# Beacon keys transposed in fp32, batch 0's first keys and queries handled apart, its last pair loaded ahead of v

## The chip, the cores and the metric

The kernel runs on one core of a Trainium2 chip. The metric is the device time of one execution in microseconds. The kernel before takes 338.09 us (median of four runs, 337.98 to 339.79). The profile shows one execution on the chip; its times are counted from the start of the execution's span.

## The reference

Causal attention with 16 extra "beacon" keys and values per head, then an MLP with a squared ReLU:

```
B, H, S, Nb, D = 8, 8, 576, 16, 64
k_all = concat([beacon_k, k], axis=2); v_all = concat([beacon_v, v], axis=2)
scores = q @ k_all.T / sqrt(D)          # beacons are seen by all, k is causal
a = softmax(scores)
attn = a @ v_all                        # (B, H, S, D)
x = attn as (B*S, H*D) = (4608, 512)
out = square(relu(x @ w_in)) @ w_out    # w_in 512 x 2048, w_out 2048 x 512
```

All inputs and the output are fp32. The kernel computes in bf16 and accumulates in fp32.

## The kernel before

The work is a pipeline of eight batches. Two heads make a pair (four pairs a batch), and their 2 x 64 columns fill TensorE's 128 rows. For a pair, q and k are brought into transposed form (`qT`, `kT`, with the 16 beacon keys first), TensorE writes scores into PSUM (line 620), ScalarE takes the exponential into `pt` (lines 629 and 671), VectorE masks the diagonal blocks by a minimum with `tri` (lines 712 and 716), TensorE multiplies with v, which has a column of ones that gives the softmax sum (line 738), and VectorE divides by that sum (lines 755 and 757). The result is transposed to `xT`: for batches 0 to 2 on TensorE (line 805) with an evacuation by ScalarE or VectorE, later by DMA (line 788). The MLP runs over nine chunks of 512 tokens: `x @ w_in` (line 901), ReLU by ScalarE or VectorE (lines 917 and 919), a square by VectorE (line 926), and `@ w_out` (line 939, the last rows line 851).

How data come in differs by batch:

- Batch 0, pair 0: two parts (240 and 336 tokens), loaded in fp32 by SP (k) and ACT (q) into `osb` (line 522), cast to bf16 by VectorE (k) and ScalarE (q), transposed on TensorE (line 481), and evacuated from PSUM by VectorE (line 327). For the first part k and q share one PSUM bank and one planned operation.
- Batch 0, pairs 1 to 3, and batch 1: loads on POOL's queue that also cast (line 449), transposed on TensorE (line 484).
- From batch 2 on: loads into staging buffers `stg` on SP's queue (lines 370 and 371), casts on POOL (line 327), and two transposing DMAs per batch (line 404).
- Beacon keys of batches 0 and 1: a load on SP (line 416), a cast to bf16 on VectorE (line 419), four small transposes on TensorE (line 429), and an evacuation into `kT` by VectorE.
- v: loads to `stg` on POOL's queue for batches 0 and 1, on SP's later, then casts into `vb` (line 327).
- Weights: DMAs with a cast on POOL's queue (lines 830 and 838), four pieces each.

The order of instructions on every engine is written at build time by a list scheduler (class `Order`). Each operation has a planned duration, a priority, dependencies, and pools that it takes from: two double PSUM strips for scores (`strip`), four PSUM banks (`ps`) for everything else, and eight staging buffers. `late` is an allowance that is added to the planned time at which TensorE may count on an operation. `behind` fixes the order of two operations. The plan only sets the order: on the chip each engine takes its instructions in that order and waits for semaphores. Until the planned 22 us, TensorE is given matmuls on zeros ("fillers", line 295) where the plan has nothing for it.

Names that the change touches: `SOFT` is the order of POOL's first loads (`p3k` is pair 3's k, `v0` a v tile, `w0` a piece of w_in, `t0` and `t1` halves of the mask). `RANK` is the order in which batch 0's eight phases (pair, part) are scored. `PLAN` says, for batches 1 to 7, how many 512-column pieces of scores are issued together: a 2 uses the two strips, a 3 two PSUM banks besides. `add_beacon` has the beacon path, `add_strided` the transposes, `add_first_loads` pair 0's loads and casts.

Of the kernel before, what the change touches and what calls it, by code (L numbers as in the profile page):

```python
# [9 lines left out]
FP32 = mybir.dt.float32  # L10
# [36 lines left out]
class Order:  # L47
# [22 lines left out]
    def run(self):  # L70
# [16 lines left out]
        free = {e: 2.3 if e == "DVE" else 0.0 for e in engines}  # L87
        dma_free = 0.0
        lanes = {"SP": [], "POOL": [], "ACT": []}
        events = [(0.0, 0, None, None)]  # L90
# [4 lines left out]
        while events:  # L95
# [19 lines left out]
            while again:  # L115
                again = False
                for e in engines:
# [26 lines left out]
                    if best is None:  # L144
                        if e == "PE" and 0.3 < now < self.FILL_UNTIL and self.pools["ps"]:
                            cols = 128 if now < 7.0 else 256
                            free[e] = now + 0.107
                            issued.append((Op("fill", "PE", 0.107, lambda e, cols=cols, bank=self.pools["ps"][0]: self.fill(bank, cols)), e, now))
                            seq += 1
                            heapq.heappush(events, (free[e], seq, "free", None))  # L150
                        continue
# [51 lines left out]
def kernel(  # L203
# [29 lines left out]
    def sb(name, shape, dt):  # L233
        return pool.tile(shape, dt, name=name)
# [32 lines left out]
    bkf = [sb("bkf", [Nb, H, D], FP32)] * 2  # L267
    bks = [sb(f"bks{i}", [Nb, H, D], BF16) for i in range(2)]
# [45 lines left out]
    ident_op = add("ident", "POOL", 1.3, lambda e: make_identity(nc, ident), prio=-300.0)  # L314
    tri_ops = [add(f"tri{i}", "POOL", (0.95, 0.55)[i], lambda e, i=i: emit_tri(e, i), prio=-250.0) for i in range(2)]
# [39 lines left out]
    def add_load(b, x, c, prio, behind=[], sync=[]):  # L355
# [34 lines left out]
        if x != "v":  # L390
            if b < NPE + 2:
                deps += [zero_ops[b]]
            else:
# [4 lines left out]
                            late=(5.0 if b else 1) if x == "v" else 0.0)  # L398

    def add_trans(b, x, prio):  # L400
        srcb, dst = (qb, qT) if x == "q" else (kb, kT)

        def emit(e):
            nc.sync.dma_start(
                out=dst[b % 2].rearrange("p g (c t) -> p (g c) t", c=NT),
                in_=srcb[b % 2].rearrange("p g c d -> p (g c d)"),
                transpose=True,
            )

        deps = [cast[b, x, c] for c in range(NT)]  # L410
        deps += [o for p in range(HP * (b - 2), HP * (b - 1)) for o in qk_ops[p]]
        trans[b, x] = [add(f"tr{b}{x}", "SP", 4.1, emit, prio=prio, deps=deps, dma=3.7, late=3.0)]

    def add_beacon(b, prio):
        prio = prio if b else -299.5
        ld = add(f"bkl{b}", "SP", 0.45, lambda e: [nc.sync.dma_start(
            out=bkf[b % 2], in_=beacon_k[b].transpose([1, 0, 2]))], prio=prio, dma=0.1,
                 deps=[cast[b - 1, "bk"]] if b else [])
        bk = add(f"bkc{b}", "DVE", 0.4, lambda e: nc.vector.tensor_copy(bks[b % 2], bkf[b % 2]), prio=prio,
                 deps=[ld])  # L420
        cast[b, "bk"] = bk
        if b:
            bk.need.extend(norm_ops[HP - 1, 0])
        box = {}

        def emit_tp(e):
            pp = ps[box["t"].held[2]].bitcast(BF16)
            for pr in range(HP):
                nc.tensor.transpose(pp[:, pr * Nb:(pr + 1) * Nb], bks[b % 2][:, 2 * pr:2 * pr + 2, :], ident[0:Nb, 0:Nb])

        busy = [o for pr in range(HP) for o in qk_ops[HP * (b - 2) + pr]] if b >= 2 else []
        box["t"] = add(f"tpb{b}", "PE", 0.25, emit_tp, prio=prio - 100.0, deps=[bk, ident_op], take=("ps", "tp"))

        def emit_ev(e):
            pp = ps[box["t"].held[2]].bitcast(BF16)
            copy_on(e, kT[b % 2][:, :, 0:Nb], pp[:, 0:HP * Nb].rearrange("p (g n) -> p g n", g=HP))

        bk_ev[b] = add(f"ekb{b}", "DVE", 0.2, emit_ev, prio=-200.0, deps=[box["t"]] + busy, give=box["t"])

    bk_ev = {}  # L440

# [17 lines left out]
    def add_strided(b, prio):  # L459
# [7 lines left out]
        for part, (t0, np_, ns, prs) in enumerate(parts_of[b]):  # L467
            n_tok = np_ * ns
            own = b == 0 and part < 2
            for pr in prs:  # L470
                groups = ["kq"] if 2 * n_tok <= 1024 else ["k", "q"]
                for n, xs in enumerate(groups):
# [20 lines left out]
                    for i, x in enumerate(xs):  # L493
# [6 lines left out]
                        if b == 0:  # L500
                            engs = ("DVE",)
                        else:
                            engs = ("DVE",) if x == "k" else ("DVE", "ACT")
                        ev = add(f"e{x}{b}.{part}.{pr}", engs,
                                 {"DVE": 0.12 + n_tok / 960.0, "ACT": 0.2 + n_tok / 1200.0}, emit_ev,
                                 prio=(-200.0 if x == "k" else -199.0) + 0.01 * part, deps=[tp])
# [5 lines left out]
    def add_first_loads():  # L512
        first = []
        at = 0
        for part in range(2):
            t0, np_, ns, _ = parts_of[0][part]
            for n, (x, t) in enumerate((("k", k), ("q", q))):
# [3 lines left out]
                def emit(e, t=t, n=n, raw=raw, t0=t0, np_=np_, ns=ns):  # L521
# [3 lines left out]
                o = add(f"fld{x}{part}", ("SP", "ACT")[n], (0.45, 0.55)[n], emit, prio=-300.0 + part,  # L525
                        dma={"k": (0.3, 0.75), "q": (0.55, 0.65)}[x][part])
                first.append(o)

                def emit_cast(e, x=x, raw=raw, part=part):
                    copy_on(e, paired_buf(x, part).rearrange("p s (u d) -> p u s d", u=2), raw)  # L530

                strided[0, part, 0, x] = add(f"fc{x}{part}", ("DVE", "ACT")[n],
                                             ((0.33, 0.75)[part], (0.42, 0.52)[part])[n], emit_cast,
                                             prio=-210.0 + part, deps=[o], late=0.3)
# [63 lines left out]
    RANK = [(0, 0), (0, 1), (1, 0), (2, 0), (1, 1), (3, 0), (2, 1), (3, 1)]  # L598
# [37 lines left out]
    PLAN = ((2,2,3,3,3),(2,2,3,3,3),(2,3,3,3,2),(2,3,3,3,2),(2,3,3,3,2),(2,3,3,3,2),(2,3,3,3,2))  # L636
# [339 lines left out]
    SOFT = "t0 p1k p1q t1 p2k p2q v0 v1 p3k p3q v2 v3 v4 w0 w1 w2 w3".split()  # L976
# [94 lines left out]
```

The softmax here doesn't subtract the row's maximum and nothing guards it: scores larger than these inputs give would overflow.

## Time and profile before

| What | Value |
|---|---|
| Median of four runs | 338.09 us (337.98 to 339.79) |
| The profiled execution | 337.98 us, its span 336.3 us |
| TensorE (PE) busy | 331.3 us, 99% of the span |
| ScalarE (ACT) busy | 191.2 us, 57% |
| VectorE (DVE) busy | 170.2 us, 51% |
| GpSimd (POOL) busy | 93.1 us, 28% |
| First scores of batch 0 start | 6.82 us |
| Last exponential of batch 0 ends | 22.98 us |
| First matmul with w_in starts | 23.12 us |
| First matmul with w_out starts | 44.37 us |

How to read it: in the busy time an engine's row gives what it executed, and a matmul's duration includes its way through the array, so consecutive matmuls overlap and a busy TensorE may still be waiting for its next instruction. "[0.58 <-PE strip L620]" behind a row says how long the engine had stood idle and what released it. The chain of work follows the last instruction back to what released it, step by step. A row of the busy time by stretches has the length, then for PE, weight loads, DVE, ACT and POOL the busy time with the number of instructions in brackets, the granted clock, the mean share of the DMA engines that is busy, and GB/s. In a row of the groups of instructions the count stands behind an x, then busy time and mean ns of one.

### The profile page before, as it was taken

The page shows a single profiled execution, that of the slowest core. Times are in us where ns is not written, and L with a number is a line of the kernel's source. Part 1 is how long each engine was busy: PE and PEld are TensorE (multiplying, and loading weights), DVE is VectorE, ACT ScalarE, POOL GpSimd, SP SyncE. Part 2 cuts the span into 40 slices and gives each one's busy share as a digit, 9 for nine tenths or more (in the row PEclk, how much of TensorE's full clock was granted, in tenths as well). Part 3 has the DMA queues.
Part 4 walks back from the last instruction along what each step waited for, and adds up shares of the span by engine and source line. Part 5 has one row for each costly group of instructions (what it writes and reads, how often), then busy time and mean ns, then how long its engine had stood idle before and what let it go on. Part 6 is the DMA issues. An engine that isn't in the chain of part 4 may idle for free.

```text
span 336.3 us, 7856 instructions
## 1 busy us (share of the span) xinstructions
PE 331.3 (99%) x3197; PEld 188.5 (56%) x3197; DVE 170.2 (51%) x389; ACT 191.2 (57%) x291; POOL 93.1 (28%) x145
## 2 busy tenths in 40 slices
PE   8999999999999999999999999999999999999996
PEld 7577765544654555555458845554555544444444
DVE  4786885248545983477147823573457302301400
ACT  3886765377647836566467556676457216515621
POOL 9874712406504614041134231424000000000000
PEclk9999999999999999999999999999999999999999
DMA  8999998999999999799699997998210231011003
GB/s 148 186 204 217 207 161 189 241 232 211 205 209 244 188 176 187 178 240 168 143 227 235 180 187 171 254 193 167 90 62 2 46 90 62 0 62 65 1 0 126
DMA packets 143955, 51.74 MB, mean 154 GB/s; under 512 B 130702, under 2 KB 138798, under 8 KB 143918
## 3 DMA queue, kind: packets, MB, share of 16 engines
q1 hardware_dynamic: 135375, 42.19, 61.5%
q0 software_dynamic: 7904, 8.69, 15.0%
q8 instruction: 25, 0.41, 0.5%
q10 hardware_dynamic: 639, 0.36, 0.4%
q14 instruction: 12, 0.10, 0.1%
HBM read 37.22 MB, written 9.44 MB: 139 GB/s over the span
## 4 chain that ended last, share of the span: by engine, by line
PE 89%; DMA 6%; POOL 4%; issue 0%; ACT 0%; POOLq 0%
PE ps L939 36%; PE ps L901 36%; PE ps L738 8%; PE strip L620 5%; DMA qk_area<-in_q_dram 4%; PE ps L620 2%; DMA stg<-in_v_dram 2%; POOL qk_area L449 1%; PE ps L851 1%; POOL w_in L830 1%; POOL vb L327 1%; PE ps L805 1%; PE ps L484 0%; POOL tri L311 0%; POOL stg L371 0%; POOL stg L370 0%
## 5 line engine op out<-in xcount | busy, mean ns | idle before, releaser
L901 PE MATMUL ps<-xT,w_in 128*128 128x512 bf16 (+3 forms) x704 | 134.3, 340 | 0.0
L939 PE MATMUL ps<-w_out,g 128*128 128x512 bf16 x560 | 130.5, 379 | 0.0
L901 PEld LDWEIGHTS <-w_in 128*128 128x128 bf16 x704 | 65.3, 98 | 51.5 <-issue 0.7
L917 ACT ACTIVATE g<-ps 128x512 bf16<-128x512 f32 (+2 forms) x118 | 66.3, 562 | 42.4 <-PE ps L901 41.8
L629 ACT ACTIVATE pt<-strip 128x1024 bf16<-128x1024 f32 (+3 forms) x86 | 81.4, 1004 | 13.2 <-PE strip L620 13.0
L926 DVE TENSOR_TENSOR g<-g 128x1024 bf16<-128x1024 bf16 (+2 forms) x80 | 52.6, 666 | 63.4 <-ACT g L917 62.4
L939 PEld LDWEIGHTS <-g 128*128 128x128 bf16 x560 | 51.6, 98 | 56.8 <-issue 1.7
L327 POOL CAST qk_area<-stg 128x512 bf16<-128x512 f32 (+2 forms) x60 | 41.4, 697 | 59.3 <-DMA stg<-in_k_dram 32.1
L325 ACT COPY osb<-ps 128x512 f32<-128x512 f32 (+2 forms) x29 | 16.4, 568 | 65.1 <-PE ps L939 60.5
L327 POOL CAST vb<-stg 128x512 bf16<-128x512 f32 (+1 forms) x40 | 26.0, 660 | 73.1 <-DMA stg<-in_v_dram 67.7
L738 PEld LDWEIGHTS <-pt 128*128 128x128 bf16 (+1 forms) x960 | 36.1, 98 | 10.2 <-DVE pt L712 0.4
L738 PE MATMUL ps<-vb,pt 128*128 128x65 bf16 (+1 forms) x960 | 39.0, 194 | 0.0
L712 DVE TENSOR_TENSOR pt<-pt,tri 128x512 bf16<-128x512 bf16 x64 | 28.4, 452 | 12.2 <-ACT pt L629 6.6
L757 DVE TENSOR_TENSOR xn<-ps,rcp 128x320 bf16<-128x320 f32 (+2 forms) x64 | 31.5, 492 | 2.3
L919 DVE TENSOR_SCALAR g<-ps 128x512 bf16<-128x512 f32 (+2 forms) x42 | 24.7, 605 | 13.1 <-PE ps L901 12.3
L671 ACT ACTIVATE pt<-ps 128x512 bf16<-128x512 f32 x42 | 22.8, 597 | 13.7 <-PE ps L620 11.1
L620 PEld LDWEIGHTS <-kT 64*128 64x128 bf16 x596 | 19.8, 94 | 16.0 <-issue 14.2
L755 DVE RECIPROCAL rcp<-ps 128x5 f32<-128x5 f32 (+2 forms) x64 | 12.2, 191 | 31.1 <-PE ps L738 30.2
L620 PE MATMUL strip<-qT,kT 64*128 64x208 bf16 (+13 forms) x474 | 27.0, 239 | 0.0
L327 DVE COPY osb<-ps 128x512 f32<-128x512 f32 (+1 forms) x9 | 5.8, 647 | 33.1 <-PE ps L939 21.3
L295 PE MATMUL ps<-g 128*128 128x128 bf16 (+1 forms) x83 | 10.6, 284 | 1.1 <-DVE warm L302 1.1
L716 DVE TENSOR_TENSOR pt<-pt,tri 80x160 bf16<-80x160 bf16 x32 | 10.8, 338 | 0.0
(42 smaller groups left out, 97.8 us busy)
## 6 DMA issues: line engine op xcount, KB each, us to landing
out_dram<-osb SPq DMA_DIRECT2D x17, 512.0 KB, 4.6
stg<-in_q_dram SPq DMA_DIRECT2D x24, 256.0 KB, 5.0
stg<-in_k_dram SPq DMA_DIRECT2D x18, 256.0 KB, 5.3
stg<-in_v_dram SPq DMA_DIRECT2D x18, 256.0 KB, 4.8
w_in<-in_moe_w_in_dram POOLq DMA_DIRECT2D x4, 512.0 KB, 7.9
w_out<-in_moe_w_out_dram POOLq DMA_DIRECT2D x4, 512.0 KB, 11.1
stg<-in_v_dram POOLq DMA_DIRECT2D x6, 256.0 KB, 7.9
stg<-in_k_dram SPq DMA_DIRECT2D x6, 224.0 KB, 4.3
```

What stands on the lines that cost most here:

```text
L327: eng[e].tensor_copy(dst, src)
L620: nc.tensor.matmul(st[hj][:, at:at + t1 - t0], kT[b % 2][hp, pr, 128 * c:128 * c + 128], qT[b % 2][hp, pr, t0:t1], start=True, stop=True,)
L629: nc.scalar.activation(pt[:, :, at:at + width], strips[qk.slots[s]][:, :, 0:width], AF.Exp, bias=0.0, scale=scale)
L671: nc.scalar.activation(pt[:, hj, at:at + 512], ps[qk.wide[hj]], AF.Exp, bias=0.0, scale=scale)
L712: nc.vector.tensor_tensor(out=d, in0=d, in1=tri[:, m0:m0 + m, :][:, None].to_broadcast([128, 2, m, 128]), op=ALU.min)
L738: nc.tensor.matmul(a[:, at + (t - tl[0]) * (D + 1):at + (t - tl[0] + 1) * (D + 1)], P[0:rr, hj, o:o + 128], vb[b % 2][0:rr, c, 2 * pr + hj ...
L757: nc.vector.tensor_tensor(out=xn[b % 2].rearrange("p t (h d) -> p h t d", d=D)[:, h0:h0 + nh, tl[0]:tl[0] + nt], in0=a[:, :, :, 0:D], in1= ...
L901: nc.tensor.matmul(h[:, lo - spans[0][0]:hi - spans[0][0]], w_in_sb[:, mc, ft * 128:(ft + 1) * 128], xT[:, mc, lo % RING:lo % RING + hi - lo],
L917: nc.scalar.activation(dst, h, AF.Relu, bias=0.0, scale=1.0)
L919: nc.vector.tensor_scalar(out=dst, in0=h, scalar1=0.0, scalar2=None, op0=ALU.max)
L926: nc.vector.tensor_tensor(out=d, in0=d, in1=d, op=ALU.mult)
L939: nc.tensor.matmul(o, G[:, fc, ts * 128:(ts + 1) * 128], w_out_sb[:, fc, :], start=(fc == 0), stop=(fc == NFT - 1))
```

## The change

- The beacon keys of batches 0 and 1 are no longer cast. TensorE transposes them in fp32 against a 16x16 fp32 identity, which VectorE makes once by a copy; the evacuation converts them to bf16. The next beacon load waits for the transposes instead of the cast, and batch 1's transposes wait for what its cast waited for. Batch 0's beacon load stands behind k's second part on SP instead of ahead of it.
- Pair 0's first part: k and q are transposed into two PSUM banks as operations of their own. The evacuation of q's second part may run on ScalarE. Some planned durations, allowances and priorities of these operations are new; pair 1 to 3's evacuations in batch 0 get a priority 500 higher, and k's second cast may run on either engine.
- Pair 3's k and q go ahead of all v tiles on POOL's queue.
- Pair 1's second phase is scored ahead of pair 2's first one.
- Batch 2's scores are issued in groups of 2 (and a last 1), without the groups of 3.
- Allowances: 3.0 instead of 5.0 for v casts of batches 1 and 2, 1.5 instead of 3.0 for batch 2's transposing DMAs.
- Fillers begin at a planned 0.9 us instead of 0.3; they widen from 128 to 256 columns at a planned 6.0 instead of 7.0. The plan for ACT starts at 0.05.

```diff
-        free = {e: 2.3 if e == "DVE" else 0.0 for e in engines}
+        free = {e: {"DVE": 2.3, "ACT": 0.05}.get(e, 0.0) for e in engines}
...
-                        if e == "PE" and 0.3 < now < self.FILL_UNTIL and self.pools["ps"]:
-                            cols = 128 if now < 7.0 else 256
+                        if e == "PE" and 0.9 < now < self.FILL_UNTIL and self.pools["ps"]:
+                            cols = 128 if now < 6.0 else 256
...
-    bkf = [sb("bkf", [Nb, H, D], FP32)] * 2
-    bks = [sb(f"bks{i}", [Nb, H, D], BF16) for i in range(2)]
+    bkf = sb("bkf", [Nb, H, D], FP32)
+    ident32 = sb("ident32", [Nb, Nb], FP32)
...
+    ident32_op = add("ident32", "DVE", 0.1, lambda e: nc.vector.tensor_copy(ident32, ident[0:Nb, 0:Nb]), prio=-300.0, deps=[ident_op])
...
-                            late=(5.0 if b else 1) if x == "v" else 0.0)
+                            late=(5.0 if b > 2 else 3.0 if b else 1) if x == "v" else 0.0)
...
-        trans[b, x] = [add(f"tr{b}{x}", "SP", 4.1, emit, prio=prio, deps=deps, dma=3.7, late=3.0)]
+        trans[b, x] = [add(f"tr{b}{x}", "SP", 4.1, emit, prio=prio, deps=deps, dma=3.7, late=3.0 if b > 2 else 1.5)]
...
-        prio = prio if b else -299.5
+        prio = prio if b else -298.5
...
-                 deps=[cast[b - 1, "bk"]] if b else [])
-        bk = add(f"bkc{b}", "DVE", 0.4, lambda e: nc.vector.tensor_copy(bks[b % 2], bkf[b % 2]), prio=prio,
-                 deps=[ld])
+                 deps=[bk_tp[b - 1]] if b else [])
...
-            pp = ps[box["t"].held[2]].bitcast(BF16)
             for pr in range(HP):
-                nc.tensor.transpose(pp[:, pr * Nb:(pr + 1) * Nb], bks[b % 2][:, 2 * pr:2 * pr + 2, :], ident[0:Nb, 0:Nb])
+                nc.tensor.transpose(ps[box["t"].held[2]][:, pr * Nb:(pr + 1) * Nb], bkf[:, 2 * pr:2 * pr + 2, :], ident32)
...
-        box["t"] = add(f"tpb{b}", "PE", 0.25, emit_tp, prio=prio - 100.0, deps=[bk, ident_op], take=("ps", "tp"))
+        box["t"] = bk_tp[b] = add(f"tpb{b}", "PE", 0.25, emit_tp, prio=prio - 100.0,
+                                  deps=[ld, ident32_op] + (norm_ops[HP - 1, 0] if b else []), take=("ps", "tp"))
...
-                groups = ["kq"] if 2 * n_tok <= 1024 else ["k", "q"]
+                groups = ["kq"] if 2 * n_tok <= 1024 and not own else ["k", "q"]
...
-                            engs = ("DVE",)
+                            engs = ("ACT", "DVE") if own and part == 1 and x == "q" else ("DVE",)
...
-                                 prio=(-200.0 if x == "k" else -199.0) + 0.01 * part, deps=[tp])
+                                 prio=(-200.0 if x == "k" else -199.0) + 0.01 * part - (500.0 if b == 0 and part == 2 else 0.0), deps=[tp])
...
-                strided[0, part, 0, x] = add(f"fc{x}{part}", ("DVE", "ACT")[n],
-                                             ((0.33, 0.75)[part], (0.42, 0.52)[part])[n], emit_cast,
-                                             prio=-210.0 + part, deps=[o], late=0.3)
+                strided[0, part, 0, x] = add(f"fc{x}{part}", (("DVE",), ("ACT",))[n] if part == 0 or x == "q" else ("ACT", "DVE"),
+                                             {"DVE": (0.46, 0.6)[part], "ACT": (0.42, 0.52)[part]}, emit_cast,
+                                             prio=-210.0 + 20.0 * part, deps=[o], late=0.1)
...
-    RANK = [(0, 0), (0, 1), (1, 0), (2, 0), (1, 1), (3, 0), (2, 1), (3, 1)]
+    RANK = [(0, 0), (0, 1), (1, 0), (1, 1), (2, 0), (3, 0), (2, 1), (3, 1)]
...
-    PLAN = ((2,2,3,3,3),(2,2,3,3,3),(2,3,3,3,2),(2,3,3,3,2),(2,3,3,3,2),(2,3,3,3,2),(2,3,3,3,2))
+    PLAN = ((2,2,3,3,3),(2,2,2,2,2,2,1),(2,3,3,3,2),(2,3,3,3,2),(2,3,3,3,2),(2,3,3,3,2),(2,3,3,3,2))
...
-    SOFT = "t0 p1k p1q t1 p2k p2q v0 v1 p3k p3q v2 v3 v4 w0 w1 w2 w3".split()
+    SOFT = "t0 p1k p1q t1 p2k p2q p3k p3q v0 v1 v2 v3 v4 w0 w1 w2 w3".split()
```

In the new order of VectorE's instructions, k's second cast stays on VectorE, and the cast of batch 0's second v tile, on POOL before, is on VectorE too.

## The prediction

> **What bounds the kernel now.** I read the page's head and its chain first.
>
> ```profile
> span 336.3 us, 7856 instructions
> ...
> PE 89%; DMA 6%; POOL 4%; issue 0%; ACT 0%; POOLq 0%
> ```
>
> From 34.45 us to the end the chain is TensorE alone, so time is won or lost by what TensorE has done by about 45 us and by new stalls after it. The chain in order of time names what holds the first part:
>
> ```profile
> 6.92 6.68 DMA stg<-in_v_dram
> 13.65 0.84 POOL vb L327
> ...
> 21.11 13.29 DMA qk_area<-in_q_dram
> 34.45 0.45 PE ps L484 x12
> ```
>
> POOL stands still for the second v tile of batch 0 until 13.65, so the first weight load is issued only at 14.43, and the queue behind it ends with batch 1's last q at 34.4. The busy time by microseconds shows the price (the last two columns are the share and rate of the DMA engines):
>
> ```profile
> 14.00:15.00 1.00, 0.66 (x16) 0.43 (x16) 0.18 (x2) 0.73 (x1) 1.00 (x2) 1.00 0.82 168
> 15.00:16.00 1.00, 1.00 (x30) 0.84 (x28) 1.00 (x2) 0.86 (x1) 1.00 (x3) 1.00 0.21 48
> 16.00:17.00 1.00, 1.00 (x13) 0.44 (x10) 0.86 (x4) 0.75 (x1) 1.00 (x2) 1.00 0.63 69
> ```
>
> The rate before and after is about 205 GB/s, so 37 + 157 + 136 = 330 KB were not moved: 330/205 = 1.6 us of an otherwise full queue. Then the timelines of ScalarE and TensorE:
>
> ```profile
> 7.19 0.78 ACT L629 ACTIVATE pt<-strip 128x736 bf16<-128x736 f32 x1 [2.12 <-PE strip L620]
> 8.56 5.00 ACT L629 ACTIVATE pt<-strip 128x832 bf16<-128x832 f32 x6 [0.58 <-PE strip L620]
> ```
>
> ```profile
> 14.34 0.45 PE L484 MATMUL ps<-ident,qk_area 96*64 96x96 bf16 x12 [0.60 <-DMA qk_area<-in_k_dram]
> ...
> 26.76 0.31 PE L805 MATMUL ps<-ident,xn 128*128 128x128 bf16 x3
> ...
> 29.72 0.70 PE L484 MATMUL ps<-ident,qk_area 96*64 96x96 bf16 x24
> ```
>
> Batch 0's 16 exponentials pace the opening: 7.19 to 22.98, with waits of 0.58, 0.23, 0.39, 0.27 and 0.50 us. Pair 3's k is late at 14.34. The 26.76 row is the last transposed piece of batch 0's output; after it TensorE has MLP work without end. The row at 29.72 starts exactly where batch 1's first k lands (issued 19.12, 10.6 us to landing), and 34.45 where its last q does.
>
> **The change, part by part.**
>
> *Start.* On SP, k's second part moves ahead of the beacon load (0.42 us): it landed at 1.74 + 3.6 = 5.34 and should at 4.9; the beacon 4.1 to 4.5. VectorE's beacon cast (0.52) goes; an identity copy of 16x16 stands in the idle time ahead of 3.40, about 0.1 by the 0.09 memset. Walking TensorE's new order: 21 fillers from 1.12 at 0.104 each end at 3.3; k's cast ends at 3.91, its two transposes at 4.2, two fillers, q's two end 4.6, four fillers 5.05, the beacon's four, six fillers, three and three transposes, first scores. The fp32 beacon transposes have no row: at least the bf16 four's 0.27 us, at most the 0.60 of L481's four with 120 columns, unless fp32 costs something the trace cannot show; I take 0.35, nearer to the same 16-column shape. First scores: 6.4 instead of 6.82. ScalarE now evacuates q's second part first (336 columns, 0.45 by its xT row of that shape), behind it waits the first exponential: 6.95 instead of 7.19. But VectorE has one evacuation less in line, so the second scores come at 7.3 and the second exponential follows the first without a gap at 7.75 instead of 8.56: 0.8 gained.
>
> *Pair 3 ahead of v.* Its two loads move from 7.81/8.45 to 5.55/6.2 on POOL; the beacon v and v tiles 0 and 1 move back past them by 1.3 us of issue. Pair 3 then lands near 10.2 and 11.4 (between q2's 9.3 and v0's 11.1, placed by bytes queued ahead) and the 0.60 wait goes. The second v tile has the same bytes ahead as pair 3's q had, which landed at 14.85: so v1 lands about 14.85 instead of 13.65. What waits: its cast is now on VectorE, ahead of the masks for pairs 1, 2 and 3 and the first norms. VectorE stands from about 14.1 to 14.85; cast to 15.45, masks to 16.85, two norms to 18.05. TensorE's first transpose of outputs is then ready at 17.5, and, in order behind it, the 14th scores go at 17.65: 0.2 of ScalarE's time. The exponentials by rows (0.75, 0.83, 0.91 start to start for 736, 832, 928) end at 21.1 instead of 22.98, one xT copy of 0.35 inside.
>
> *After the last exponential* TensorE is short, not ScalarE: four long AV groups of 0.75, six output transposes of 0.15 and the next beacon's 0.2, 4.1 us, still lie between its last scores (20.0) and a free run, against 2.3 behind its last scores (22.0) before. So only 0.7 of the 1.9 us remains: the last such transpose ends near 24.95 with 3 of the nine 240-column L901 groups before it done, worth 24.95 + 3 x 0.41 = 26.2 against 26.9.
>
> *The queue.* POOL now issues all v and the first weight load (near 11.7) before it waits for v, so the DMA dip closes: 1.6 us earlier at most for w_in, batch 1's q and k, w_out and batch 2; 1.2 to 1.6, I take 1.5. TensorE comes to batch 1's first transposes at 28.9 (landing 28.2), to the one at 34.45 by 33.4 (landing 32.9). The stalls before these rows shrink (0.2 and 0.5 us of 7.9), so the 0.7 becomes 1.4. The two gains are one: the same stream, first bound by TensorE, then by arrival. w_out's parts, landing at 42.4, 44.9, 46.5, 49.2, move alike and stay ahead of L939 (44.37 before, 42.9 now).
>
> *Batch 2 in twos* takes seven visits to the scores instead of five. After a visit 12 L901 matmuls take 2.70 us against 12 x 0.216 = 2.60: 0.1 each, +0.2. ScalarE saves three pairs of halves (2 x 0.60) for three of 1.00, off the path. Its output products come some 4.5 us sooner in the order; their v casts end at 80.36 less 1.5 = 78.9, their place is near 81.0. The shorter allowances move batch 3's first scores two L939 groups forward, 102.34 - 1.4 - 1.7 = 99.2; the transposed k lands at 92.17 + 7.1 = 99.3 less 1.5. Both fit, by 2 and 1.4 us.
>
> Two beacon casts and one evacuation leave VectorE: nothing, since VectorE is 51% busy and TensorE has MLP groups to run; if that cover failed, 0.46 us each.
>
> Sum: -1.4 + 0.2 = -1.2. The profiled run took 337.98 us for a span of 336.3; the new span is 335.1, and with the same 1.7 around it 336.8. The median of the four is 338.09, 0.1 above that run. Half a percent (1.7 us) is about what timing this kernel can tell from no change.
>
> [...] The fillers show TensorE's warm-up:
>
> ```profile
> L295 PE MATMUL ps<-g 128*128 128x128 bf16 x13 | 1.6, 311 | 0.0
> ```
>
> ```profile
> L295 PE MATMUL ps<-g 128*128 128x128 bf16 x12 | 1.1, 249 | 0.0
> ```
>
> (3 to 4 us, and 5.8 to 6.4 us.) The granted clock reads 1.00 all along, yet a 128-column filler takes 311 ns before 5.8 and 249 after. [...] The change opens a hole from 3.3 to 3.95, 11 fillers fewer ahead of the first transposes. [...]
>
> **Rivals.** (1) *Gain stays under 0.5% because v is late*: each microsecond that the second v tile lands beyond 14.85 goes through VectorE's queue into the 14th scores; the third tile landed 2 us behind the second in the old mix (15.7), so 1 us late is possible. Then batch 0 gains nothing and only the closed dip remains, behind TensorE: -0.3 +/- 0.5, 337.7. For it: VectorE is already busy 0.92 or more in six of the seven microseconds from 17. (2) *More than 0.5%*: from 23.1 to 44.4 the groups' start-to-start times add up to 19.7 of 21.25 us, and from there to 101.4 to 55.9 of 57.0: of these 2.7 the -1.4 has counted some 0.5; with half of the rest gone too it is -2.3, 335.7, with all of it -3.4, 334.6. Against it: part of them is ScalarE's and VectorE's evacuation of PSUM (3.9 us of ScalarE's waits there are for L901, so it isn't full). (3) *Slower*: batch 3's scores (or batch 2's products) are placed before their data; TensorE takes its list in order, so it stands. Batch 3's margin is 1.4 us: if the transposed k comes later than that, all beyond it is lost. One k transpose took 7.1 us from issue where the median is 5.7; a loss of that 1.4 in three batches is +4.2 - 1.2, 341. Against it: the order past batch 3 has the old shape and the old allowance of 3.0. (4) *The opening doesn't get earlier*, if fp32 transposes or fillers push the first scores to 6.8: the second exponential then loses 0.4 of the 0.8: 337.2.
>
> **How the numbers follow.** The forecast with rival 4 has 0.37 (its own range 336.1 to 337.6, of which 0.04 lies under 336.4, half a percent below the median); rival 1 0.10; rival 2 0.35; rival 3 0.18, of which 0.15 beyond 339.8. So faster by over 0.5% 0.39, within 0.46, slower 0.15. The range goes down to rival 2's further end, 334.6, and up to 340.0, which leaves out some 0.06 below and 0.13 above.
>
> **What would show it.** Right: second exponential near 7.8; no DMA share under 0.8 between 14 and 17; last exponential's end near 21; batch 1's last q landing near 32.9; first L939 near 42.9; the chain all TensorE from 33. Wrong: fillers above 300 ns after 6 us; VectorE waiting on v beyond 15; TensorE waits on qT or kT of batch 3 near 99.

## The result, and the profile after

| | Before | Changed |
|---|---|---|
| Median | 338.06 us (64 executions, 337.19 to 340.12) | 339.58 us (43 executions, 338.09 to 344.93) |
| Profiled execution, its span | 337.98 us, 336.3 us | 338.73 us, 337.0 us |

The ratio is 1.0041, with a 95% interval of 1.0032 to 1.0051. The forecast was 336.8 us, a gain of 1.2 us; the change lost 1.5 us. The profiled execution of the changed kernel lies 0.85 us under its median: only 5 of the 43 were faster. What that hides came out in the experiments.

The head and the chain of the changed kernel answer to the lines that carried the prediction:

```profile
span 337.0 us, 7821 instructions
...
PE 95%; DVE 2%; DMA 1%; issue 1%; SPq 0%; ACT 0%; DVEq 0%
```

GpSimd has left the chain, but TensorE only has a larger share of a longer span. In the timeline of TensorE (start, duration, count behind the x, idle time and what ended it in brackets) the opening goes as predicted:

```profile
1.12 2.42 PE L295 MATMUL ps<-g 128*128 128x128 bf16 x21 [1.12 <-DVE warm L302]
3.68 0.38 PE L477 MATMUL ps<-ident,qk_area 120*128 120x120 bf16 x2
...
5.14 0.42 PE L424 MATMUL ps<-ident,bkf 16*128 16x16 f32 x4 [0.45 <-DMA bkf<-in_beacon_k_dram]
5.49 0.51 PE L295 MATMUL ps<-g 128*128 128x128 bf16 x6
...
6.22 0.33 PE L616 MATMUL strip<-qT,kT 64*128 64x240 bf16 x4
6.49 0.72 PE L295 MATMUL ps<-g 128*128 128x256 bf16 x5
```

There are 21 fillers, a hole of 0.14 us behind them, another of 0.45 us where the beacon keys are late, and the first scores at 6.22. ScalarE's timeline shows four exponentials without a gap from 6.66, and the last one ending at 21.32 (before: 22.98):

```profile
6.66 3.58 ACT L625 ACTIVATE pt<-strip 128x736 bf16<-128x736 f32 x4
10.49 8.60 ACT L625 ACTIVATE pt<-strip 128x736 bf16<-128x736 f32 x10 [0.25 <-PE strip L616]
...
20.45 0.87 ACT L625 ACTIVATE pt<-strip 128x832 bf16<-128x832 f32 x1
```

The busy time by microseconds, 14 to 17 us, shows that the dip of the DMA engines has closed too (last two columns; 0.82, 0.21 and 0.63 before):

```profile
14.00:15.00 1.00, 1.00 (x12) 0.59 (x11) 0.46 (x2) 0.87 (x2) 1.00 (x2) 1.00 0.95 199
15.00:16.00 1.00, 1.00 (x12) 0.51 (x9) 1.00 (x4) 0.96 (x2) 0.88 (x3) 1.00 1.05 179
16.00:17.00 1.00, 1.00 (x19) 0.56 (x17) 0.64 (x3) 1.00 (x2) 0.95 (x1) 1.00 1.25 208
```

What did not follow is the rest. GpSimd's timeline has a new wait for v0, the weights' last piece at 18.42 and batch 1's first k at 19.16, where before it was issued at 19.12 (first row, from the kernel before):

```profile
19.12 0.70 POOL L449 DMA_DIRECT2D qk_area<-in_k_dram  x1
```

```profile
13.79 0.61 POOL L328 CAST vb<-stg 128x512 bf16<-128x512 f32 x1 [1.40 <-DMA stg<-in_v_dram]
...
18.42 0.75 POOL L826 DMA_DIRECT2D w_in<-in_moe_w_in_dram  x1
19.16 0.69 POOL L445 DMA_DIRECT2D qk_area<-in_k_dram  x1
```

That k landed 10.8 us later, at 29.97 (before 29.72); the last q at 34.45 (before 34.40). TensorE starts on the k at once, and then stands where it did not stand before:

```profile
30.02 0.70 PE L480 MATMUL ps<-ident,qk_area 96*64 96x96 bf16 x24 [0.44 <-ACT g L913]
...
40.28 0.40 PE L616 MATMUL ps<-qT,kT 64*128 64x192 bf16 x6 [0.17 <-DVE g L915]
...
43.48 1.03 PE L897 MATMUL ps<-xT,w_in 128*128 128x272 bf16 x8 [0.50 <-DVE g L915]
...
45.73 2.75 PE L935 MATMUL ps<-w_out,g 128*128 128x512 bf16 x12
```

**A ledger of TensorE's losses.** Where two kernels order the work differently, one place can't be compared with one place. So for each profile I count the work done: every matmul but the fillers at one fixed price for its shape, as in unbroken runs (0.216 us for 512 columns, fewer columns in proportion, about 0.031 us for the 65 columns of a product with v; the two heads' scores, which start 4 ns apart, count once), some 311 us in either kernel. A group's start less the work ahead of it is what TensorE has lost by then. Where the order differs, a mark falls into another group, so that single columns of two such kernels agree to some 0.1 us only. The profiles below are those of the experiments; "behind 24" lies near 39 us of the span, 30 near 45, 62 near 78, 80 near 97.

| Lost behind so much work (us) | 8 | 24 | 30 | 62 | 80 | end | profiled time |
|---|---|---|---|---|---|---|---|
| before | 13.28 | 14.84 | 15.05 | 16.01 | 16.76 | 22.02 | 337.98 |
| changed | 13.10 | 14.39 | 15.49 | 16.31 | 17.54 | 22.76 | 338.73 |
| changed, profiled again (e13) | 15.63 | 16.41 | 16.61 | 17.44 | 18.50 | 23.73 | 339.76 |
| changed, a third time (e14) | 14.88 | 15.66 | 16.46 | 17.28 | 18.35 | 23.57 | 339.53 |
| changed, more fillers (e5) | 13.35 | 14.48 | 15.43 | 16.26 | 17.40 | 22.63 | 338.59 |
| changed, v first again (e8) | 12.52 | 14.39 | 14.60 | 15.41 | 16.48 | 21.69 | 337.64 |
| fillers, v first, threes (e17) | 12.78 | 14.10 | 14.50 | 15.45 | 16.31 | 21.39 | 337.36 |

The differences at the end agree with those of the times (+0.74 against +0.75, +1.71 against +1.78, -0.63 against -0.62), so the ledger holds all of it, and nearly all of it arises before 97 us.

### The profile page after: what moved, and what is told of

It is laid out like the page before. It is cut to its first block, busy times and chain, and to the rows that moved or that the text cites. A ratio compares the mean times of both kernels' runs of the same rounds, so it can differ in the third digit from the quotient of the medians.

```text
span 337.0 us, 7821 instructions
## 1 busy us (share of the span) xinstructions
PE 331.1 (98%) x3187; PEld 187.4 (56%) x3187; DVE 170.5 (51%) x388; ACT 191.3 (57%) x289; POOL 92.3 (27%) x144
## 4 chain that ended last, share of the span: by engine, by line
PE 95%; DVE 2%; DMA 1%; issue 1%; SPq 0%; ACT 0%; DVEq 0%
PE ps L935 36%; PE ps L897 36%; PE ps L734 9%; PE strip L616 6%; PE ps L616 2%; PE ps L295 2%; PE ps L480 1%; PE ps L801 1%; PE ps L847 1%; DMA bkf<-in_beacon_k_dram 1%; DVE g L915 1%; DVE g L922 1%; DVE qT L328 0%; DVE xn L753 0%; SPq L518 0%
## 5 line engine op out<-in xcount | busy, mean ns | idle before, releaser
L913 ACT ACTIVATE g<-ps 128x512 bf16<-128x512 f32 (+2 forms) x122 | 68.7, 564 | 50.5 <-PE ps L897 48.4
L625 ACT ACTIVATE pt<-strip 128x1024 bf16<-128x1024 f32 (+3 forms) x89 | 84.5, 1003 | 20.4 <-PE strip L616 19.8
L922 DVE TENSOR_TENSOR g<-g 128x1024 bf16<-128x1024 bf16 (+2 forms) x80 | 55.0, 693 | 67.2 <-ACT g L913 66.3
L326 ACT COPY osb<-ps 128x512 f32<-128x512 f32 (+2 forms) x26 | 14.6, 566 | 49.3 <-PE ps L935 45.8
L616 PE MATMUL strip<-qT,kT 64*128 64x112 bf16 (+14 forms) x490 | 28.0, 239 | 0.0
L915 DVE TENSOR_SCALAR g<-ps 128x512 bf16<-128x512 f32 (+2 forms) x38 | 22.1, 594 | 8.6 <-PE ps L897 8.3
L667 ACT ACTIVATE pt<-ps 128x512 bf16<-128x512 f32 x36 | 19.5, 598 | 11.7 <-PE ps L616 10.4
L328 DVE COPY osb<-ps 128x512 f32<-128x512 f32 (+1 forms) x12 | 7.9, 658 | 35.4 <-PE ps L935 23.5
L295 PE MATMUL ps<-g 128*128 128x256 bf16 (+1 forms) x73 | 10.2, 279 | 1.1 <-DVE warm L302 1.1
L372 POOL DMA_DIRECT2D stg<-in_v_dram x10 | 8.5, 871 | 6.1 <-DMA w_in<-in_moe_w_in_dram 5.1
```

What stands on the lines that cost most here:

```text
L328: eng[e].tensor_copy(dst, src)
L616: nc.tensor.matmul(st[hj][:, at:at + t1 - t0], kT[b % 2][hp, pr, 128 * c:128 * c + 128], qT[b % 2][hp, pr, t0:t1], start=True, stop=True,)
L625: nc.scalar.activation(pt[:, :, at:at + width], strips[qk.slots[s]][:, :, 0:width], AF.Exp, bias=0.0, scale=scale)
L667: nc.scalar.activation(pt[:, hj, at:at + 512], ps[qk.wide[hj]], AF.Exp, bias=0.0, scale=scale)
L913: nc.scalar.activation(dst, h, AF.Relu, bias=0.0, scale=1.0)
L915: nc.vector.tensor_scalar(out=dst, in0=h, scalar1=0.0, scalar2=None, op0=ALU.max)
```

## The experiments

### Each part alone or undone

**e1_weights_early**: only the DMA dip of the kernel before is closed, by a first weight load ahead of the last v tile.

```diff
-    SOFT = "t0 p1k p1q t1 p2k p2q v0 v1 p3k p3q v2 v3 v4 w0 w1 w2 w3".split()
+    SOFT = "t0 p1k p1q t1 p2k p2q v0 v1 p3k p3q v2 v3 w0 v4 w1 w2 w3".split()
```

> The kernel before with one edit: the first piece of w_in goes onto POOL's queue ahead of batch 0's last v tile, so that the queue is no longer empty at 15 to 17 us; pair 3 stays behind v. Theory of the prediction (the empty stretch is lost queue time): the DMA share at 15 to 17 us rises above 0.8, batch 1's first k lands 1.2 to 1.6 us earlier than 29.7 and its last q earlier than 34.4 by as much, and the time falls by 0.5 to 1.4 us. Rival (the empty stretch is the tail of a few DMA engines that hold what everything later waits for, or the arrivals are bound by when they are issued): the share rises, yet batch 1's arrivals stay within 0.4 us of 29.7 and 34.4, and the time stays within 0.4 us of before or gets worse.

Measured: 339.04 us (338.41 to 340.83), ratio 1.0036 [1.0017, 1.0054]. The busy time by microseconds:

```profile
15.00:16.00 1.00, 1.00 (x29) 0.71 (x25) 1.00 (x2) 0.97 (x2) 1.00 (x3) 1.00 1.22 202
16.00:17.00 1.00, 1.00 (x12) 0.56 (x11) 0.83 (x5) 0.94 (x2) 1.00 (x3) 1.00 1.23 202
```

The dip is closed. Only batch 1's first k is issued earlier (17.24 us); the other three loads go 0.2 us later than before. Its first k transposes start at 29.55, 0.2 us earlier than before, and the last q lands 1.1 us earlier, at 33.3. No gain came of it: the last v tile is now cast at 19.43, behind a wait of 1.49, and TensorE's loss in the opening had grown by over 1 us behind 8 us of work. From 14 to 17 us 517 KB were moved, 232 more than before, 1.1 us at 205 GB/s: the closed gap brought the last q that much forward, the first k by 0.2 us only, and what closed it was wanted elsewhere.

**e2_twos_alone**: only batch 2 in twos, in the kernel before. **e3_threes_back**: the changed kernel without them.

```diff
-    PLAN = ((2,2,3,3,3),(2,2,3,3,3),(2,3,3,3,2),(2,3,3,3,2),(2,3,3,3,2),(2,3,3,3,2),(2,3,3,3,2))
+    PLAN = ((2,2,3,3,3),(2,2,2,2,2,2,1),(2,3,3,3,2),(2,3,3,3,2),(2,3,3,3,2),(2,3,3,3,2),(2,3,3,3,2))
```

> The kernel before with batch 2's scores in twos and nothing else. If the seven visits to the scores cost what the trace after shows between 66 and 104 us, +0.4 us; by the prediction's price +0.2; if ScalarE's fewer half pieces free TensorE's PSUM banks, a gain of 0.3.

> The changed kernel with batch 2's scores in threes again; the order up to batch 1's end stays as in the changed kernel. If the twos carry most of the loss, the time falls by 0.8 us or more, to 338.7; by the loss seen in the trace after, by 0.4; if the loss lies in the opening and in batch 1, by less than 0.2.

Measured: e2 338.36 us, ratio 1.0000 [0.9974, 1.0026]; e3 339.30 us, ratio 1.0025 [1.0008, 1.0042]. The twos do not explain the loss alone: by its session's median of the kernel before (337.77) e2 is 0.6 us slower, and its interval leaves room for 0.9 us either way. But the profile of e3 was of another kind than that of the changed kernel, although nothing differs ahead of batch 2 (TensorE's timeline):

```profile
7.35 0.49 PE L616 MATMUL strip<-qT,kT 64*128 64x240 bf16 x4
7.77 1.25 PE L295 MATMUL ps<-g 128*128 128x256 bf16 x5
8.95 0.53 PE L616 MATMUL strip<-qT,kT 64*128 64x336 bf16 x4
```

The same five fillers that took 0.72 us now take 1.25, and the first scores start 1.13 us later. This made the theory of the next group: in some executions the array is still "cold" at 7 to 9 us and runs these fillers at about half its rate ((1.25 - 0.41)/4 = 0.21 us start to start, 411 ns each), where in others it is "warm" ((0.72 - 0.27)/4 = 0.11 us, 274 ns each).

**e4_allowances_back**: the changed kernel with the old allowances.

```diff
-                            late=(5.0 if b > 2 else 3.0 if b else 1) if x == "v" else 0.0)
+                            late=(5.0 if b else 1) if x == "v" else 0.0)
...
-        trans[b, x] = [add(f"tr{b}{x}", "SP", 4.1, emit, prio=prio, deps=deps, dma=3.7, late=3.0 if b > 2 else 1.5)]
+        trans[b, x] = [add(f"tr{b}{x}", "SP", 4.1, emit, prio=prio, deps=deps, dma=3.7, late=3.0)]
```

> The changed kernel with the old allowances (5.0 us for v casts of batches 1 and 2, 3.0 for batch 2's transposes). Theory that the shorter allowances make TensorE stand for late data: 0.5 to 1.5 us faster, and the spread of the times (338.1 to 344.9) shrinks to that of before (337.2 to 340.1). Rival, that the data come in time anyway and the loss is in draining PSUM at 38 to 44 us: within 0.4 us of the changed kernel, the same spread.

Measured: 339.25 us (338.15 to 344.81), ratio 1.0026 [1.0006, 1.0045]: no cause can be told here either. Its profile too had 256-column fillers of 411 ns up to 8.2 us.

**e8_v_first_again**: the changed kernel with pair 3 behind the first two v tiles.

```diff
-    SOFT = "t0 p1k p1q t1 p2k p2q p3k p3q v0 v1 v2 v3 v4 w0 w1 w2 w3".split()
+    SOFT = "t0 p1k p1q t1 p2k p2q v0 v1 p3k p3q v2 v3 v4 w0 w1 w2 w3".split()
```

> The changed kernel with v tiles 0 and 1 ahead of pair 3 again on POOL's queue. By the prediction's price the second v tile lands 1.2 us earlier and VectorE doesn't stand for it, but pair 3 is late as before: +0.3 to +0.8 us over the changed kernel. If loading pair 3 early gains nothing because batch 1's arrival takes the lead back: within 0.3 us. Theory W says nothing of it beyond its spread, since the fillers stay.

Measured: 339.20 us (337.64 to 341.50), ratio 1.0040 [1.0019, 1.0060]. By its median pair 3's place is worth nothing that can be told. Its profiled execution, its fastest, took 337.64 us, and the ledger shows where: 0.2 instead of 1.1 us lost between 24 and 30. Both readings are taken up below.

**e7_batch1_first**: the kernel before with batch 1's q and k issued ahead of the last two pieces of w_in.

```diff
-    SOFT = "t0 p1k p1q t1 p2k p2q v0 v1 p3k p3q v2 v3 v4 w0 w1 w2 w3".split()
+    SOFT = "t0 p1k p1q t1 p2k p2q v0 v1 p3k p3q v2 v3 v4 w0 w1".split()
...
-    v_loads[1][0].behind[:] = [strided[1, 0, HP - 1, "q"]]
+    w_ops["in", 2].behind[:] = [strided[1, 0, HP - 1, "q"]]
+    w_ops["in", 3].behind[:] = [w_ops["in", 2]]
+    v_loads[1][0].behind[:] = [w_ops["in", 3]]
```

> The kernel before with batch 1's four q and k loads moved ahead of the last two pieces of w_in on POOL's queue. If batch 1's arrival at 29.7 to 34.4 us is what holds TensorE in this stretch, these loads land some 5 us sooner (1 MB at 205 GB/s), TensorE's lost time between 26 and 45 us (1.7 us before) falls by 0.5 to 1 and the total by as much; if the pieces of w_in, now 5 us later, or the draining of PSUM hold it as much, the total stays within 0.4 us or rises.

Measured: 337.86 us, ratio 0.9995 [0.9980, 1.0011]. The four loads are issued 1.7 us earlier (the first k at 17.40), and TensorE starts on that k at 27.83 instead of 29.72. Batch 1's arrival, even when pulled forward by the order of the queue, is worth nothing that can be told.

### The fillers

**e9_before_21_fillers** tests the number of fillers alone: the kernel before, with the first 11 of its 32 opening fillers left out and every other instruction in its place. The fillers multiply zeros into a bank that nobody reads, so no part of the result is left out.

```diff
+        skip = 11
         for op, e, _ in issued:
+            if op.name == "fill" and skip:
+                skip -= 1
+                continue
             if e != "-":
```

> The kernel before with the first 11 of its fillers left out, so that 21 stand ahead of the first transposes as in the changed kernel; nothing else moves. TensorE is then idle from 3.3 to 4.4 us. [...] Rival (the fillers' number doesn't matter, e5's gain came from elsewhere): within 0.3 us of before.

Measured: 339.64 us (338.13 to 341.88), ratio 1.0055 [1.0024, 1.0086]: 1.4 us over its session's kernel before (338.28), as much as the change lost, from the fillers alone. The groups of TensorE's instructions from 6.2 to 7.2 us (count, busy time, mean ns of one), first of this kernel, then of the kernel before:

```profile
L299 PE MATMUL ps<-g 128*128 128x128 bf16 x8 | 1.1, 314 | 0.0
```

```profile
L295 PE MATMUL ps<-g 128*128 128x128 bf16 x9 | 0.8, 220 | 0.0
```

That the fillers cost this much is shown; how, this profile does not show. TensorE stood for 0.61 us behind the 21 fillers, the array was cold to about 9 us, and still this execution took 338.40 us, 0.1 over the kernel before. Against the profile before, TensorE was 1.36 us behind at the second scores, 0.69 when pair 3's k had come (14.3 us, where the kernel before waits) and 0.23 from 35 us on. The median comes from slower executions: five of the twelve took 341.0 to 341.9 us, and none of these was profiled.

**e5_more_fillers**: the changed kernel with fillers from a planned 0.3 us again (26 instead of 21 fit, as the first transposes come earlier), and five of 128 columns ahead of batch 0's beacon transposes. No other instruction moves.

```diff
-                        if e == "PE" and 0.9 < now < self.FILL_UNTIL and self.pools["ps"]:
+                        if e == "PE" and 0.3 < now < self.FILL_UNTIL and self.pools["ps"]:
...
         def emit_tp(e):
+            for _ in range(5 if b == 0 else 0):
+                emit_fill(box["t"].held[2], 128)
             for pr in range(HP):
```

> The changed kernel with fillers alone added: 26 instead of 21 ahead of the first transposes, and five more right ahead of the beacon's fp32 transposes, where TensorE stood for the beacon load; every other instruction keeps its place. Theory W (with the fewer fillers TensorE, in a share of the executions, isn't yet warm at 6 us, fillers of 256 columns then take 411 ns and the opening loses 1.6 to 2.4 us): always warm by 7, the median falls by 0.8 to 1.5 us from the changed kernel's 339.6, and the spread shrinks to that of before. Rival A (the loss is batch 1's data arriving unchanged and PSUM drained late at 38 to 44 us): less than 0.3 us change, the same spread.

Measured: 338.54 us (337.55 to 339.78), ratio 1.0011 [0.9991, 1.0031], so 1.0 us less than the changed kernel's median. It is still 0.7 us over its session's kernel before (337.85), where the forecast was 1.2 under: the fillers are not all of the miss. Its fillers ran at 221 ns from 5.5 us on, and both holes are gone from the timeline:

```profile
1.12 2.96 PE L295 MATMUL ps<-g 128*128 128x128 bf16 x26 [1.12 <-DVE warm L302]
3.97 0.38 PE L479 MATMUL ps<-ident,qk_area 120*128 120x120 bf16 x2
...
5.39 0.41 PE L426 MATMUL ps<-ident,bkf 16*128 16x16 f32 x4
```

**e6_fewer_fillers**: the kernel before with the new threshold alone, 26 instead of 32 fillers.

```diff
-                        if e == "PE" and 0.3 < now < self.FILL_UNTIL and self.pools["ps"]:
+                        if e == "PE" and 0.9 < now < self.FILL_UNTIL and self.pools["ps"]:
```

> The kernel before with 26 instead of 32 fillers ahead of the first transposes; every other instruction keeps its place. Theory W: in a share of the executions the first warm matmuls come after 7 us instead of 6, and the median rises by 0.5 to 1.2 us with a wider spread. Rival A: within 0.3 us of before.

Measured: 338.28 us (337.50 to 340.56), ratio 1.0016 [0.9999, 1.0033]: by the medians six fillers fewer cost 0.4 us (its session's kernel before took 337.85; the interval runs from nothing to 1.1), eleven cost 1.4.

**e13_changed_again, e14_changed_again**: the changed kernel, profiled twice more.

> The changed kernel itself, one further profile. Theory W: fillers at 311 ns until either 4 to 6 us (a time near 338.2) or 8 to 10 us (near 339.5 or more); two of the four profiles with its opening were of the second kind. Rival: always warm by 6 us.

> As the run before it: another profile of the changed kernel, either warm by 6 us with a time near 338.2, or at 8 to 10 us with a time near 339.5 or more.

Measured: 339.76 and 339.53 us, at the changed kernel's median, where its first profile was not. TensorE's timeline of e13:

```profile
3.97 0.38 PE L477 MATMUL ps<-ident,qk_area 120*128 120x120 bf16 x2 [0.43 <-DVE qk_area L328]
...
5.44 0.61 PE L424 MATMUL ps<-ident,bkf 16*128 16x16 f32 x4 [0.25 <-DMA bkf<-in_beacon_k_dram]
5.98 0.82 PE L295 MATMUL ps<-g 128*128 128x128 bf16 x6
6.59 0.77 PE L477 MATMUL ps<-ident,qk_area 112*128 112x112 bf16 x6
7.29 0.49 PE L616 MATMUL strip<-qT,kT 64*128 64x240 bf16 x4
7.71 1.25 PE L295 MATMUL ps<-g 128*128 128x256 bf16 x5
```

The groups from 7.2 to 8.2 us, of e13 and then of the changed kernel's first profile:

```profile
L295 PE MATMUL ps<-g 128*128 128x256 bf16 x3 | 0.8, 412 | 0.0
```

```profile
L295 PE MATMUL ps<-g 128*128 128x256 bf16 x3 | 0.7, 276 | 0.0
```

In e13 the array is cold past 9 us (406 ns from 9 to 10), in e14 to about 9 (421, then 294). The ledger prices it: 2.53 and 1.78 us lost behind 8 us of work against the warm profile of the same instructions, 0.97 and 0.81 at the end. The granted clock reads 1.0 and 0.999 in the two: it does not show this.

Six profiles have the changed kernel's opening with its 21 fillers. The array was warm by 4.2 us in its first one (338.73 us) and by 5.1 in e8 (337.64), and cold to about 9 us or later in the other four (e3, e4, e13, e14: 339.25 to 339.76). What differs ahead of that is how long TensorE stands behind the 21 fillers for k's first cast: 0.14 and 0.18 us in the warm two, 0.42 to 0.51 in the cold four, where this cast ended 0.25 to 0.4 us later. TensorE's row in e8 (that of e13 stands above):

```profile
3.72 0.38 PE L477 MATMUL ps<-ident,qk_area 120*128 120x120 bf16 x2 [0.18 <-DVE qk_area L328]
```

That this hole decides is not shown: no run set its length, and e16 below was cold without it.

### After the fillers: what else the change did

**e10_fillers_and_threes**: e5 with batch 2 in threes again. **e11_fillers_and_q_on_scalar**: e5 with batch 1's q evacuations on ScalarE only, because two of them stand ahead of the ReLUs that TensorE waits for at 40 to 43 us.

```diff
-                            engs = ("DVE",) if x == "k" else ("DVE", "ACT")
+                            engs = ("DVE",) if x == "k" else ("ACT",)
```

> The changed kernel with the fillers of e5 and batch 2's scores in threes. By TensorE's lost time in the warm profiles (0.74 us more than before in all, 0.4 of it in batch 2) the time falls by 0.4 from e5 to 338.1, level with before; if the twos cost nothing, as their run on the kernel before suggests, it stays at 338.5.

> The changed kernel with the fillers of e5 and all evacuations of batch 1's q on ScalarE; in the changed kernel two of the four (0.76 us each, at 36.1 us) stand on VectorE ahead of ReLUs that TensorE waits for at 43.5. If these are what takes the lead back, TensorE's lost time between 38 and 46 us falls by 0.5 or more and the time by as much from e5 to about 338.0; if batch 1's arrivals alone set the pace, no change from 338.5.

Measured: e10 338.03 us, ratio 0.9987 [0.9966, 1.0008]; e11 338.39 us, ratio 1.0004 [0.9980, 1.0027]. Threes are 0.5 us faster than twos here (338.54) by the medians and 0.8 by the ratios, and the intervals overlap. In e11 the loss between 24 and 30 was 0.2 instead of 0.95 us, but 0.87 came back behind 34 to 36 of work, where TensorE now waits 0.52 us for a part of w_out to land (row at 49.66), so moving the evacuations gained little.

**e12_fillers_batch1_first**: e15's kernel (below) with e7's order of the weights.

> The changed kernel with the fillers of e5, v tiles ahead of pair 3 again, batch 1's q and k ahead of the last two pieces of w_in, and threes: it keeps the new opening (beacon, k and q apart) and takes away each cost found so far. If the opening's lead of 0.3 us then survives and the stretch to 46 us loses 0.5 less, 337.0 to 337.6, better than before; if other waits take the lead's place, 337.9 to 338.4.

Measured: 339.16 us (338.43 to 340.31), ratio 1.0026 [1.0005, 1.0047]. A miss, with an array that was warm at 5.5 us, and 1.8 us behind the profile of e15. Part of it is the meeting told of below: four of VectorE's squares took 3.12 us from 37.26, beside GpSimd's casts, and TensorE then waited 0.86 us for VectorE. No run tested it, and e7's order is no gain to build on.

**e15_fillers_v_first_threes, e17_v_first_threes_again**: e5 with v first and threes. **e16_fillers_threes_allowances**: e10 with the old allowances. **e18_nine_fillers**: e15 with nine fillers ahead of the beacon transposes.

> The changed kernel with the fillers of e5, v tiles 0 and 1 ahead of pair 3, and threes: what is left of the change is the opening of pair 0 and the allowances. If loading pair 3 early is worth nothing, the same time as e10 within 0.4 us (338.0); if it is worth the 0.5 us that the opening's trace suggests, 338.5.

> The changed kernel with the fillers of e5, threes and the old allowances. If the shorter allowances cost anything, faster than e10's 338.0 by 0.3 or more; if not, the same within 0.4.

> The changed kernel with 26 fillers first, five fillers ahead of the beacon transposes, v first again and batch 2 in threes: what measured 337.42 us, ratio 0.9986 [0.9964, 1.0007], once more over more executions. If it is a real gain over the kernel before, the ratio stays near 0.998 and its interval lies under 1; if the earlier median was luck, about 338.0 and a ratio near 1.000, like the same kernel with pair 3 first (338.03).

> The same kernel with nine fillers instead of five ahead of the beacon transposes (4 x 0.105 to 4 x 0.157 = 0.4 to 0.6 us more work there). The five did not always do: one profile of this kernel had 314 ns fillers until 6.2 us, a sister of it until 7.2. If a thin filler budget is still costing in some executions, the upper values (338.5 to 340.1) thin out and the median falls by some 0.2 us although the first scores come 0.4 us later in a warm execution. If warm-up is no longer the issue, the median is equal or up to 0.4 us higher.

Measured: e15 337.42 us, 0.9986 [0.9964, 1.0007]; e17, the same kernel, 337.42 us, 0.9975 [0.9951, 1.0000]; e16 338.52 us, 1.0012 [0.9996, 1.0028]; e18 337.86 us, 0.9987 [0.9959, 1.0015]. So what is left of the change, when kept warm, is perhaps 0.2% faster than the kernel before, at the edge of what can be told. Nine fillers at the beacon bring no gain over five that can be told. By its median e16 shows no gain from the old allowances. Five fillers are not always enough: e16's profile, the slowest of its twelve executions at 339.90 us, was cold to about 10 us, where the other six profiles with these five were warm by 7:

```profile
8.07 1.25 PE L295 MATMUL ps<-g 128*128 128x256 bf16 x5
```

In e17 TensorE reaches w_out at 44.73:

```profile
29.74 0.70 PE L482 MATMUL ps<-ident,qk_area 96*64 96x96 bf16 x24 [0.25 <-DMA qk_area<-in_k_dram]
...
44.73 2.54 PE L937 MATMUL ps<-w_out,g 128*128 128x512 bf16 x10
```

**Where the 1.1 us between 24 and 30 goes.** The chain of the changed kernel names VectorE's squares (line 922) near 40 us. Their rows, and those of GpSimd's v casts for batch 1, in the changed kernel:

```profile
38.80 1.08 DVE L922 TENSOR_TENSOR g<-g 128x480 bf16<-128x480 bf16 x1
...
40.16 1.97 DVE L922 TENSOR_TENSOR g<-g 128x544 bf16<-128x544 bf16 x3
```

```profile
37.88 1.73 POOL L328 CAST vb<-stg 128x512 bf16<-128x512 f32 x3
...
40.49 1.35 POOL L328 CAST vb<-stg 128x512 bf16<-128x512 f32 x2
```

and the same squares in e13, where the casts ran from 37.01 to 38.74 and from 39.61 to 40.77:

```profile
40.83 0.40 DVE L922 TENSOR_TENSOR g<-g 128x480 bf16<-128x480 bf16 x1
41.49 1.15 DVE L922 TENSOR_TENSOR g<-g 128x544 bf16<-128x544 bf16 x3
```

The first square of the changed kernel begins beside the casts and ends about 0.3 us after the third of them; one that begins behind the casts takes 0.40. Of the three in its second row, the one that begins ahead of the next casts, at 40.16, takes 0.42, and the two that begin beside them, at 40.50 and 41.28, take 0.86 and 0.84. Over 0.40 and 1.15 the squares here took 1.5 us more in the changed kernel, 1.35 in e5, 1.2 in e10, 1.0 in e14, 0.4 in e17, 0.2 in e8 and none in e13. The ledger's loss from 24 to 30 runs 1.10, 0.95, 0.78, 0.80, 0.40, 0.21 and 0.20. That the casts are what makes the squares longer is read from seven profiles with this order of squares, and was not tried by moving the casts; why they would, no run shows.

The meeting itself is not new. In the kernel before five squares took 1.89 and 1.16 us in the same place, 1.15 more than undisturbed, and yet the ledger's loss from 24 to 30 is 0.21:

```profile
37.98 1.89 DVE L926 TENSOR_TENSOR g<-g 128x544 bf16<-128x544 bf16 x3
...
41.12 1.16 DVE L926 TENSOR_TENSOR g<-g 128x480 bf16<-128x480 bf16 x2
```

So here a longer square cost only where TensorE waited for what VectorE does behind it, as it did in the changed order (the wait of 0.50 us at 43.48). What brings the casts there is open. The start of the first three does not decide: it is 37.88 in the changed kernel, but 37.32 in e10, which lost 0.78, and 37.34 and 37.40 in e8 and e17, which lost little. The fourth cast comes at 39.92 to 40.49 in the three warm profiles with pair 3 first and q's evacuations in their old place (the changed kernel, e5, e10), and earlier, by 39.5, in the two with v first.

## Why the prediction was wrong

- **"The queue"** (-1.4, the opening's 0.7 among it and the whole gain of the forecast) is the step that failed in all three profiles of the changed kernel, warm or cold. The dip closed as said, but batch 1's arrivals stayed (29.97 for 29.72, 34.45 for 34.40), and TensorE came to w_out at 45.73 instead of the 42.9 of the forecast. The prediction took bytes not moved in a gap for time gained at the end of the queue. GpSimd's queue got its gap back as a 1.40 us wait for v0, so the loads behind it were issued when they had been before. The busy time by microseconds shows another part: from 4 to 14 us the DMA engines moved 1.82 MB, 0.2 MB less than before, so most of the 0.3 MB won at 14 to 17 had been lost ahead of it. And where arrival did come earlier, it bought no time: 0.2 to 1.1 us in e1, 1.9 us in e7.
- **The paragraph on the fillers** holds the second step that failed. It saw the hole and counted 11 fillers fewer, but the sum of -1.2 has no price for either. Its row (249 ns at 5.8 to 6.4 us) was of a kernel with 32 fillers and said nothing of 21. What the runs showed: cold to about 9 us in four of six profiles with this opening, 1.4 us for the fillers alone (e9), 1.0 us back with fillers added (e5), and 0.8 to 1.0 us of a cold opening left at the end of e13 and e14. The 21 fillers are 2.42 us of work, and the array was warm at 4.2 us in one execution and cold past 9 in another: how much work it takes to be warm, and by when, no run shows.
- **"Start"** and **"Pair 3 ahead of v"** were right in a warm execution: first scores 6.22 for 6.4, the late v cast at 14.69 for 14.85, the last exponential's end 21.3 for 21.1. The fp32 beacon transposes took 0.35 us start to start, as taken. Rivals 1 and 4 fall with that.
- **"After the last exponential"** promised 0.7 us; the ledger has 0.45 behind 24 of work in the warm profile. A size, not a mechanism.
- **What pair 3 ahead triggers** was followed into VectorE's queue at 14 to 18 us, not further. What TensorE lost between 24 and 30 of work, 1.1 us in the first profile, read as the meeting of squares and v casts near 40 us, stood in no term and no rival.
- **Batch 2 in twos** (+0.2): in the ledger from 62 to 80, 1.06 to 1.23 us with twos and 0.75 and 0.86 with threes, so +0.2 to +0.5: the right sign, and a size at or above the forecast. No wait on batch 3's data appeared, so rival 3, the one that ended slower, had the right sign for the wrong reason.
- The range held the median, and of the signs shown as wrong ("fillers above 300 ns after 6 us") the first is what e13 and e14 show.

By the ledger the first profile's +0.74 is -0.45 (opening), +0.89 (24 to 30, read as squares beside casts), -0.14 (30 to 62), +0.48 (62 to 80, twos among it) and -0.04. A cold array puts e13 and e14 0.8 to 1.0 above that, which is the median's +1.5. Not explained: five of the 43 executions lay between 342 and 345 us, as did one of e3 and three of e4, and e9 has five above 341; none of them was profiled. So it is shown that fewer fillers cost time; that a cold array is all of that cost is not.

## What to carry to other kernels

Where a change touches the start of TensorE's work, count what keeps the array busy there (11 fillers fewer cost 1.4 us in e9) and read its warmth from the duration of a repeated matmul in several executions (here 406 to 421 ns cold and 276 warm); one profile can be the lucky one. Count a closed gap in a DMA queue only once the later loads are seen to land earlier and something is seen to wait for them (here the first k landed at 29.97 for 29.72). When an engine's work moves, look beside the new waits also for instructions of VectorE that get longer beside GpSimd's casts (here a square of 1.08 us for 0.40), and ask whether TensorE now waits behind them.

## What was not expected of the hardware

- The granted clock reads 1.0 while 256-column matmuls take 406 to 421 ns instead of 276, and 128-column ones 314 instead of 221. In these traces only the durations tell.
- The same order with 21 fillers led to a warm array at 4.2 us in one execution and to a cold one to about 9 us or later in others; the hole behind the fillers was 0.14 us in the one and 0.42 to 0.51 in the others.
- Of the 1.8 to 2.5 us that a cold start costs by 8 us of work, 0.8 to 1.0 is left at the end: 0.5 is won back at 30 us, where the warm execution stands before batch 1's first transposes, and 0.7 at 43.5, where it waits for VectorE.
- A square of 0.40 us took up to 1.44 (e14) beside casts of 0.58 us each on another engine, with no wait in its row: the row itself is longer.
